# Moving one half tile's Relu and product into a later gate step of a fused state-space and ReGLU kernel

## The chip, the cores and the metric

The kernel runs on one core of a Trainium2 chip. The metric is the device time of one execution in microseconds. Three timed executions of the kernel before took 121.81, 121.49 and 121.47 us; their median is 121.49 us.

## The reference

Two stages follow each other. The first is a chunked state-space layer over `x` (4 batches, 8 heads, 768 positions, 32 channels) with a decay `a` and projections `B`, `C` of 16 states. For every chunk `c`:

```python
cum = np.cumsum(la, axis=-1)                       # la = log a of the chunk
M = (C_c @ B_c.T) * exp(cum_i - cum_j) * causal    # within the chunk
y = M @ x_c + (C_c @ state) * exp(cum)             # and from what came before
state = exp(sum la) * state + sum_j exp(cum_end - cum_j) * B_j x_j
```

The second stage takes the result as 3072 tokens of 256 channels through a gated feed-forward layer:

```python
gate = np.maximum(x @ w_gate, 0.0)     # 256 -> 1536
val = x @ w_val                        # 256 -> 1536
out = (gate * val) @ w_out             # 1536 -> 256
```

## The kernel before

The first stage works in pairs of 128-position chunks (256 tokens a pair, twelve pairs), the second in blocks of 512 tokens (two pairs a block, six blocks). A block has twelve gate steps `f`, one for each 128 columns of the 1536, and then output matmuls `o` (L810) that sum over the twelve. The work of both stages is woven together by hand: the order of the Python calls is the order on every engine's queue, and a last pass (`in_order`) pins each engine to it. There is no scheduler. What an instruction waits for follows from the tiles it reads and from the buffer it reuses.

A pair needs these steps. `transp` (L410) turns B and C, `bevac` and `cevac` (L415 to L436) copy them out of PSUM as `BT` and `CT`. `G` (L473) makes the products of C and B in four banks, and `gevac` copies them out with the causal mask: two of the copies by ScalarE (L486, L494), the rest by VectorE (L497). `back` (L454) turns `BT` back into a PSUM tile `bt`, in the bank that `transp` had used, so it waits until the last copy of `CT` has read that bank. `x_cast` makes `xb`, x in bf16. `astep` (L531) adds to the running state `A_ps`, `sevac` copies it out (`Sd`, L545, by ScalarE, or `carry` and `Sm`, L560 and L568, by VectorE). `Dm` (L652) multiplies the masked products with `xb`, `inter` (L632) adds the part of the state, and `yevac` writes the result `y` to `yT` in halves (ScalarE and VectorE).

A gate step of a whole block (`gv`, L765 to L769) is two matmuls into a bank `gate` and two into a bank `val`, a Relu by ScalarE (L768) that writes `r`, and a product by VectorE (L769) that writes a slice of `h`. Steps 0 to 3 of block 0 are done in halves of 256 tokens (`gvh_mm`, `gvh_relu`, `gvh_mul`, L780 to L792), with gate and val in one bank: the first halves (u = 0) while pair 1 is still in its first stage, the second halves (u = 1) as soon as pair 1 is in `yT`. Steps 4 to 11 follow as whole steps. Within step 5 comes `over_sum` (VectorE), after step 7 `sevac(1, 1)` (two VectorE instructions), after step 9 `turn` and `tevac` of pair 2 (PE transposes, one ScalarE copy, two VectorE scalings), after step 11 `back` of pair 2, and then the first output matmuls.

PSUM has eight banks. Five are shared by one pool tag and given to whatever asks next (`bank`); the tag "y" is a single bank, used by the warm-up matmuls, by the `y` of some pairs, and here by the half tile of step 0. The tile `r` has four buffers.

The lines that the change touches, in the order of the calls around them:

```python
gevac(1, early=True, between=lambda: backevac(1, nc.scalar))
gvh_relu(0, 0, 0)
for i in range(2):
    x_cast(1, i, nc.scalar)
```

Of the kernel before, what the change touches and what calls it, by code (L numbers as in the profile page):

```python
# [8 lines left out]
FP32 = mybir.dt.float32  # L9
# [20 lines left out]
def kernel(  # L30
# [31 lines left out]
    mm = ctx.enter_context(tc.tile_pool(name="mm", bufs=1, space=bass.MemoryType.PSUM))  # L62
# [3 lines left out]
    def bank(name="bank", shape=(128, 512), dtype=FP32):  # L66
        return mm.tile(list(shape), dtype, tag="shared", bufs=NSHARED, name=name)
# [89 lines left out]
    def w_tile(ws, f, k):  # L157
        return ws[f // 2][:, k, f % 2:256:2]
# [102 lines left out]
    def over_sum(de):  # L261
        own = smask.rearrange("p t (q d) -> p (t q) d", q=4)[:, :, 0]
        prod = const.tile([128, NB, 8], FP32)
        nc.vector.tensor_tensor(
            out=prod, in0=de.rearrange("p (b h) -> p b h", b=NB),
            in1=own.rearrange("p (o h) -> p o h", o=1).to_broadcast([128, NB, 8]),
            op=ALU.mult)
        nc.vector.tensor_reduce(out=over, in_=prod, op=ALU.add, axis=mybir.AxisListType.X)
# [187 lines left out]
    def backevac(p, eng):  # L456
        s = st[p]
        bx = att.tile([128, 2, 128], BF16, tag="bx", name="bx", bufs=4)
        copy(eng, bx, s.pop("bt"))
        s["B"] = [bx[:, i] for i in range(2)]  # L460
# [19 lines left out]
    def gevac(p, half=True, early=False, between=None, after={}):  # L480
        s = st[p]
        g = [t.rearrange("j i t m -> j (i t) m") for t in s["gp"]]
        d = s["gs"]
        wide = p < NWIDE
        m = masks[:, int(wide):int(wide) + 1].to_broadcast([128, 4, 128])
        nc.scalar.copy(out=d[:, 0], in_=g[0])  # L486
        causal(d[:, 0], 4, wide)
        if between:
            between()
        h = 2 if half else 0  # L490
        if early:
            nc.vector.tensor_tensor(out=d[:, 1, 0:2], in0=g[1][:, 0:2], in1=m[:, 0:2],
                                    op=ALU.mult)
        nc.scalar.copy(out=d[:, 1, h:4], in_=g[1][:, h:4])  # L494
        causal(d[:, 1, h:4], 4 - h, wide)
        for q in (2, 3):
            nc.vector.tensor_tensor(out=d[:, q], in0=g[q], in1=m, op=ALU.mult)  # L497
            if q in after:
                after[q]()
        if half and not early:  # L500
            nc.vector.tensor_tensor(out=d[:, 1, 0:2], in0=g[1][:, 0:2], in1=m[:, 0:2],
                                    op=ALU.mult)
# [19 lines left out]
    def astep(p, i):  # L522

        c = 2 * (p % PPB) + i
        if c == NC - 1:
            return
        if not A_ps:
            A_ps.append(mm.tile([128, 2, 128], FP32, tag="Aps", name="A_ps"))
        xi = st[p]["x"][i].rearrange("s (t q d) -> s q t d", t=2, q=4)
        for q in range(4):  # L530
            nc.tensor.matmul(  # L531
                out=A_ps[0][32 * q:32 * q + 32, 0, 0:64].rearrange("p (t d) -> p t d", t=2),
                lhsT=st[p]["B"][i][:, 32 * q:32 * q + 32], rhs=xi[:, q],
                start=(c == 0 or c == NC - 2), stop=True, tile_position=(0, 32 * q),
                skip_group_check=True)
# [3 lines left out]
    def sevac(p, i):  # L539
        c = 2 * p + i + 1  # L540
        if c == NC:
            return
        if c < 2 * NTILE:
            S[c] = n = att.tile([128, 64], BF16, tag="Sd", name="Sd")
            nc.scalar.copy(out=n, in_=A_ps[0][:, 0, 0:64])  # L545
        else:
            S[c] = spread_one(c, 0)
# [7 lines left out]
    def spread_one(c, k):  # L555

        b, a = c // NC, A_ps[0][:, 0, 64 * k:64 * k + 64]
        if c % NC == NC - 2:
            n = carried[b] = att.tile([128, 64], FP32, tag="carry", name="carry", bufs=2)
            nc.vector.tensor_scalar_mul(n, a, over[:, b:b + 1])  # L560
            a = n
        elif c % NC == NC - 1:
            n = att.tile([128, 64], FP32, tag="carry2", name="carry2", bufs=2)
            nc.vector.tensor_tensor(out=n, in0=a, in1=carried[b], op=ALU.add)
            a = n
        n = att.tile([128, 2, 128], BF16, tag="Sm", name="Sm", bufs=5)
        a = a.rearrange("p (t o d) -> p t o d", t=2, o=1)
        nc.vector.tensor_tensor(  # L568
            out=n.rearrange("p t (q d) -> p t q d", q=4),
            in0=a.to_broadcast([128, 2, 4, D]),  # L570
            in1=smask.rearrange("p t (q d) -> p t q d", q=4), op=ALU.mult)
        return n
# [91 lines left out]
    def yevac(p, *engs):  # L664
        s = st.pop(p)
        dst = yT[:, :, p * 256:(p + 1) * 256]
        if p >= NWIDE:
            copy(engs[0], dst.rearrange("q t (i m) -> q t i m", i=2), s["ya"])
            return
        for t in range(2):  # L670
            copy(engs[t % len(engs)],
                 dst[:, t].rearrange("q (i m r) -> q i r m", i=2, r=2),
                 s["y"][t].rearrange("q i (r m) -> q i r m", r=2))
# [84 lines left out]
    def gv(b, f, turns=False):  # L758
        if b not in fst:
            fst[b] = ffn.tile([128, NF, 512], BF16, tag="h", name="h")  # L760
        tk = slice(b * 512, (b + 1) * 512)
        g, v = bank("gate"), bank("val")
        order = [(g, wgs, 0), (g, wgs, 1), (v, wvs, 0), (v, wvs, 1)]
        for o, ws, k in sorted(order, key=lambda e: e[2]) if turns else order:
            nc.tensor.matmul(out=o, lhsT=w_tile(ws, f, k), rhs=yT[:, k, tk],  # L765
                             start=(k == 0), stop=(k == 1), skip_group_check=True)
        r = ffn.tile([128, 512], BF16, tag="r", name="r", bufs=4)
        nc.scalar.activation(r, g, AF.Relu)  # L768
        nc.vector.tensor_tensor(out=fst[b][:, f], in0=r, in1=v, op=ALU.mult)  # L769

    def gvh_mm(b, f, u):
        if f == 0 and u == 0:
            fst[b] = ffn.tile([128, NF, 512], BF16, tag="h", name="h")
        tk = slice(b * 512 + u * 256, b * 512 + (u + 1) * 256)
        gv_ = (mm.tile([128, 2, 256], FP32, tag="y", name="gv") if b + f == 0 else
               bank("gv", (128, 2, 256)))
        jk = [(j, k) for j in range(2) for k in range(2)]
        early = b + f + u == 0
        for j, k in sorted(jk, key=lambda v: v[1]) if early else jk:
            nc.tensor.matmul(out=gv_[:, j], lhsT=w_tile((wgs, wvs)[j], f, k), rhs=yT[:, k, tk],  # L780
                             start=(k == 0 and not (early and j)), stop=(k == 1),
                             skip_group_check=True)
        fst[b, f, u] = gv_

    def gvh_relu(b, f, u):
        fst[b, f, u, "r"] = r = ffn.tile([128, 512], BF16, tag="r", name="r", bufs=4)
        nc.scalar.activation(r[:, 0:256], fst[b, f, u][:, 0], AF.Relu)  # L787

    def gvh_mul(b, f, u):
        nc.vector.tensor_tensor(  # L790
            out=fst[b][:, f, u * 256:(u + 1) * 256], in0=fst.pop((b, f, u, "r"))[:, 0:256],
            in1=fst.pop((b, f, u))[:, 1], op=ALU.mult)  # L792
# [158 lines left out]
    G(1)  # L951
    back(1)
    gevac(1, early=True, between=lambda: backevac(1, nc.scalar))
    gvh_relu(0, 0, 0)
    for i in range(2):
        x_cast(1, i, nc.scalar)
    weights(3, (1,))
# [20 lines left out]
    inter(1, 0)  # L978
    inter(1, 1)
    astep(1, 1)  # L980
    gvh_mul(0, 0, 0)
    yevac(1, nc.scalar, nc.vector)
    gvh_relu(0, 2, 0)
    gvh_mm(0, 3, 0)
# [13 lines left out]
    for b in range(NBLK):  # L998
# [44 lines left out]
        for f in range(nh, NF):  # L1043
            gv(b, f, b > 2 and f == 0)
            if b == 0:
                if f == 5:
                    over_sum(de_ps)
                if f == 7:
                    sevac(1, 1)
                if f == 9:  # L1050
                    turn(P)
                    tevac(P, nc.scalar, nc.vector)
                if f == 10:
                    held(Q, bc=False)
                if f == 11:
                    back(P)
                    backevac(P, nc.scalar)
            elif b == 1:
                if f == 8:
                    scale_padded(Q + 1, nc.gpsimd)  # L1060
                    load(Q + 3, nc.sync)
            elif b == 2:
                if f == 9:
                    load(Q + 3, nc.sync)
            elif b == 3:
                if f in (2, 6):
                    scale(P + 2 + f // 4, nc.gpsimd)
# [142 lines left out]
```

## Time and profile before

| | |
|---|---|
| median of three runs | 121.49 us (121.47 to 121.81) |
| the profiled execution, its own time | 121.42 us |
| span from its first to its last instruction | 119.7 us |
| granted TensorE clock | 1.00 |
| busy: PE, VectorE, ScalarE, GpSimd | 96%, 73%, 64%, 43% of the span |

The time of an execution is 1.72 us above the span, which lies around the program's instructions. A row of the timeline has the start in us, the length in us, the engine, the line of the kernel, the operation, what is written from what is read, the shapes, and the number of instructions that the row merges; in brackets stands how long the engine was idle before and who released it. PEld is the loading of weights for PE. Instructions on one engine overlap: the next one starts before the one ahead has ended, so lengths do not add up and the distance between starts is what one costs.

### The profile page before, as it was taken

What the parts mean: (1) busy time and instruction counts of PE and PEld (TensorE: products, weight loads), DVE (VectorE), ACT (ScalarE), POOL (GpSimd) and SP (SyncE); (2) the same over time, 40 slices, a digit from 0 to 9 for tenths busy, and PEclk for the clock granted to TensorE, in tenths of its full rate; (3) what the DMA queues carried; (4) which work ended last, traced back from release to release, by engine and by line L of the source; (5) the groups of instructions that cost most, each with busy time, mean ns of one, the idle gap of its engine ahead of it and who ended that gap; (6) DMA issues with size and microseconds to landing.
All of it is one profiled execution on the core that took longest, in us unless ns stands there. A gap on an engine that the chain in (4) does not pass through costs nothing.

```text
span 119.7 us, 3291 instructions
## 1 busy us (share of the span) xinstructions
PE 115.0 (96%) x1222; PEld 74.6 (62%) x1229; DVE 87.1 (73%) x202; ACT 77.0 (64%) x168; POOL 51.2 (43%) x104
## 2 busy tenths in 40 slices
PE   7989999999999999999999999999999999999990
PEld 2446754677884577887578544578444677444790
DVE  6896779976898767899765778756787775678400
ACT  4288986777997635888627776535766445767240
POOL 7878999744413363957046635133400033000000
PEclk9999999999999999999999999999999999999999
DMA  3999999989999999999799999992200002200022
GB/s 67 212 176 182 203 198 205 202 121 129 93 117 132 144 127 135 101 104 177 72 175 118 97 128 218 267 312 93 88 0 5 0 0 93 88 0 0 0 88 88
DMA packets 82675, 14.22 MB, mean 119 GB/s; under 512 B 75500, under 2 KB 82660, under 8 KB 82660
## 3 DMA queue, kind: packets, MB, share of 16 engines
q1 hardware_dynamic: 75172, 11.07, 59.5%
q0 software_dynamic: 4080, 2.36, 14.0%
q10 hardware_dynamic: 3408, 0.59, 2.6%
q8 instruction: 9, 0.15, 0.5%
q14 instruction: 6, 0.05, 0.1%
HBM read 11.13 MB, written 3.15 MB: 119 GB/s over the span
## 4 chain that ended last, share of the span: by engine, by line
PE 95%; ACT 1%; issue 0%; DVE 0%
PE o L810 26%; PE gate L765 19%; PE val L765 19%; PE gv L780 14%; PE w L200 4%; PE g L513 2%; PE g L473 2%; PE y L705 1%; PE y L652 1%; PE o L822 1%; PE A_ps L237 1%; PE tp L410 1%; PE y L641 1%; ACT CT L434 1%; PE bt L454 1%; PE y L692 0%
## 5 line engine op out<-in xcount | busy, mean ns | idle before, releaser
L769 DVE TENSOR_TENSOR h<-r,val 128x512 bf16<-128x512 bf16 x54 | 36.9, 687 | 9.6 <-ACT r L768 7.5
L768 ACT ACTIVATE r<-gate 128x512 bf16<-128x512 f32 x54 | 32.3, 597 | 12.2 <-PE gate L765 11.7
L810 PE MATMUL o<-wo,h 128*128 128x256 bf16 x276 | 33.8, 273 | 0.0
L765 PE MATMUL gate<-yT,wg 128*128 128x512 bf16 x105 | 32.0, 379 | 0.2
L765 PE MATMUL val<-yT,wv 128*128 128x512 bf16 x105 | 31.5, 379 | 0.2
L810 PEld LDWEIGHTS <-h 128*128 128x128 bf16 x276 | 25.7, 98 | 5.4 <-issue 1.2
L171 POOL TENSOR_SCALAR_AFFINE_SELECT gs<-gs 128x512 bf16<-128x512 bf16 (+1 forms) x24 | 12.1, 527 | 28.4 <-ACT gs L486 28.4
L497 DVE TENSOR_TENSOR gs<-g,masks 128x512 bf16<-128x512 f32 x24 | 15.4, 685 | 5.9 <-PE g L513 2.8
L765 PEld LDWEIGHTS <-wv 128*128 128x128 bf16 x108 | 10.6, 98 | 12.4
L765 PEld LDWEIGHTS <-wg 128*128 128x128 bf16 x108 | 10.5, 98 | 11.5
L790 DVE TENSOR_TENSOR h<-r,gv 128x256 bf16<-128x256 bf16 x36 | 14.2, 417 | 1.3 <-ACT r L787 1.1
L787 ACT ACTIVATE r<-gv 128x256 bf16<-128x256 f32 x36 | 13.7, 390 | 1.2
L486 ACT CAST gs<-g 128x512 bf16<-128x512 f32 x12 | 7.0, 587 | 11.2 <-PE g L513 5.8
L780 PE MATMUL gv<-yT,wg 128*128 128x256 bf16 x72 | 13.9, 273 | 0.2 <-ACT yT L339 0.2
L780 PE MATMUL gv<-yT,wv 128*128 128x256 bf16 x72 | 13.8, 272 | 0.0
L842 ACT COPY ob<-o 128x512 f32<-128x512 f32 x11 | 6.5, 591 | 4.3 <-PE o L810 3.9
L299 POOL TENSOR_TENSOR bz<-bcr,fac 128x512 bf16<-128x512 f32 x6 | 6.4, 1060 | 5.6 <-PE gate L765 3.1
L339 ACT CAST yT<-y 128x256 bf16<-128x256 f32 (+1 forms) x11 | 5.4, 516 | 4.5 <-PE y L705 2.7
L780 PEld LDWEIGHTS <-wv 128*128 128x128 bf16 x72 | 7.0, 98 | 1.1 <-issue 0.3
L780 PEld LDWEIGHTS <-wg 128*128 128x128 bf16 x72 | 6.8, 98 | 1.0 <-issue 0.2
L339 POOL CAST xb<-xr 128x512 bf16<-128x512 f32 (+1 forms) x8 | 4.7, 591 | 4.2 <-DMA xr<-in_x_dram 4.0
L200 PE MATMUL w<-const-bfloat16-1.0 128*128 128x512 bf16 (+3 forms) x14 | 5.2, 498 | 0.8 <-PEq L1194 0.8
(120 smaller groups left out, 108.4 us busy)
## 6 DMA issues: line engine op xcount, KB each, us to landing
xr<-in_x_dram SPq DMA_DIRECT2D x24, 128.0 KB, 3.1
out_dram<-ob SPq DMA_DIRECT2D x11, 256.0 KB, 2.6
bcr<-in_B_dram SPq DMA_DIRECT2D x16, 64.0 KB, 2.9
bcr<-in_C_dram SPq DMA_DIRECT2D x16, 64.0 KB, 2.9
wg<-in_moe_w_gate_dram POOLq DMA_DIRECT2D x6, 128.0 KB, 4.5
wv<-in_moe_w_val_dram POOLq DMA_DIRECT2D x6, 128.0 KB, 4.7
wo<-in_moe_w_out_dram POOLq DMA_DIRECT2D x3, 256.0 KB, 6.8
bcr<-in_B_dram SPq DMA_DIRECT2D x3, 128.0 KB, 5.6
```

The lines of the kernel that those rows point to most:

```text
L171: nc.gpsimd.affine_select(out=dst, in_=dst, pattern=pattern, compare_op=ALU.is_ge, fill=0.0, base=0, channel_multiplier=-1)
L200: nc.tensor.matmul(out=w[:, 0:cols], lhsT=nc.const_aps.tensor(1.0, [128, 128], BF16), rhs=nc.const_aps.tensor(1.0, [128, cols], BF16), sta ...
L339: (eng.copy if eng is nc.scalar else eng.tensor_copy)(out=out, in_=in_)
L486: nc.scalar.copy(out=d[:, 0], in_=g[0])
L497: nc.vector.tensor_tensor(out=d[:, q], in0=g[q], in1=m, op=ALU.mult)
L765: nc.tensor.matmul(out=o, lhsT=w_tile(ws, f, k), rhs=yT[:, k, tk], start=(k == 0), stop=(k == 1), skip_group_check=True)
L768: nc.scalar.activation(r, g, AF.Relu)
L769: nc.vector.tensor_tensor(out=fst[b][:, f], in0=r, in1=v, op=ALU.mult)
L780: nc.tensor.matmul(out=gv_[:, j], lhsT=w_tile((wgs, wvs)[j], f, k), rhs=yT[:, k, tk], start=(k == 0 and not (early and j)), stop=(k == 1), ...
L787: nc.scalar.activation(r[:, 0:256], fst[b, f, u][:, 0], AF.Relu)
L790: nc.vector.tensor_tensor(out=fst[b][:, f, u * 256:(u + 1) * 256], in0=fst.pop((b, f, u, "r"))[:, 0:256], in1=fst.pop((b, f, u))[:, 1], op ...
L810: nc.tensor.matmul(out=o[:, ts % 2], lhsT=fst[b][:, f, ts * 128:(ts + 1) * 128], rhs=wo[:, f], start=(f == 0 and new), stop=(f == NF - 1), ...
```

## The change

Three things are edited. The Relu of the half tile (0, 0, 0) leaves its place ahead of the two casts of x of pair 1 and comes after step 7 of block 0; its product leaves its place ahead of the copy of `y` and comes after step 8. So that the half tile can keep the bank of the tag "y" until then, the second half of step 0 (u = 1) takes a shared bank instead of that one. No instruction is added or removed, and the order of PE's, GpSimd's and the DMA queues' instructions is the same.

```diff
-        gv_ = (mm.tile([128, 2, 256], FP32, tag="y", name="gv") if b + f == 0 else
+        gv_ = (mm.tile([128, 2, 256], FP32, tag="y", name="gv") if b + f + u == 0 else
                bank("gv", (128, 2, 256)))
...
     gevac(1, early=True, between=lambda: backevac(1, nc.scalar))
-    gvh_relu(0, 0, 0)
     for i in range(2):
         x_cast(1, i, nc.scalar)
...
     astep(1, 1)
-    gvh_mul(0, 0, 0)
     yevac(1, nc.scalar, nc.vector)
...
                 if f == 7:
                     sevac(1, 1)
+                    gvh_relu(0, 0, 0)
+                if f == 8:
+                    gvh_mul(0, 0, 0)
                 if f == 9:
                     turn(P)
                     tevac(P, nc.scalar, nc.vector)
```

## The prediction

> **What bounds the kernel now.** I read the page first, then the chain of waits, then the timeline around the two places that the edit touches, engine by engine.
>
> ```profile
> span 119.7 us, 3291 instructions
> PE 115.0 (96%) x1222; PEld 74.6 (62%) x1229; DVE 87.1 (73%) x202; ACT 77.0 (64%) x168; POOL 51.2 (43%) x104
> PE 95%; ACT 1%; issue 0%; DVE 0%
> 13.50:22.80 9.30, 9.25 (x59) 5.30 (x57) 8.43 (x21) 7.46 (x20) 9.30 (x14) 1.00 1.44 205
> ```
>
> TensorE is busy for 96% of the span and holds 95% of the chain that ended last. The last row is a stretch from the table by stages (length, then busy PE, PEld, DVE, ACT, POOL, the granted clock, DMA): through the gate steps of block 0 PE is busy 9.25 of 9.30 us at full clock. PE's order is not changed, so the question is only where PE would wait less and where it would wait more. What shifts PE here shifts the end, since I see nothing behind it that PE waits for long enough to absorb it. The first place is the end of pair 1's first stage:
>
> ```profile
> 11.44 0.39 ACT L494 CAST gs<-g 128x256 bf16<-128x256 f32 x1
> 11.70 0.41 ACT L787 ACTIVATE r<-gv 128x256 bf16<-128x256 f32 x1
> 11.98 0.73 ACT L339 CAST xb<-xr 128x256 bf16<-128x256 f32 x2
> 12.72 0.21 ACT L545 CAST Sd<-A_ps 128x64 bf16<-128x64 f32 x1
> 12.10 0.30 PEld L258 LDWEIGHTS dall<-pick,ends 96*128 96x128 f32 x2
> 12.44 0.11 PEld L531 LDWEIGHTS <-bx 128*32 128x32 bf16 x4
> 12.76 0.18 PEld L652 LDWEIGHTS <-xb 128*32 128x32 bf16 x12 [0.18 <-ACT xb L339]
> 12.46 0.21 PE L531 MATMUL A_ps<-xb,bx 128*32 128x64 bf16 x4
> 12.48 0.63 PE L652 MATMUL y<-gs,xb 128*32 128x128 bf16 x16
> 13.04 0.40 PE L632 MATMUL y<-CT,Sd 32*32 32x128 bf16 x16
> 13.50 0.45 DVE L339 CAST yT<-y 128x256 bf16<-128x256 f32 x1 [0.62 <-PE y L632]
> ```
>
> The Relu that moves is the second row. Behind it stand the two casts of x, which end at 11.98 + 0.73 = 12.71, and twelve of the sixteen weight loads of L652 wait for the second cast until 12.76. That is a real wait of PE on ScalarE. The second place is the end of the gate steps:
>
> ```profile
> 20.17 0.28 DVE L560 TENSOR_SCALAR carry<-A_ps,over 128x64 f32<-128x64 f32 x1
> 20.48 0.42 DVE L568 TENSOR_TENSOR Sm<-carry,smask 128x256 bf16<-128x256 f32 x1
> 20.83 1.28 DVE L769 TENSOR_TENSOR h<-r,val 128x512 bf16<-128x512 bf16 x2
> 22.02 0.60 DVE L436 TENSOR_SCALAR CT<-tp,tmask 128x256 bf16<-128x256 bf16 x2
> 22.54 0.68 DVE L769 TENSOR_TENSOR h<-r,val 128x512 bf16<-128x512 bf16 x1
> 22.41 0.10 PEld L765 LDWEIGHTS <-wv 128*128 128x128 bf16 x1
> 22.74 0.20 PEld L454 LDWEIGHTS <-BT 128*128 128x128 bf16 x2 [0.23 <-issue]
> 22.41 0.59 PE L765 MATMUL val<-yT,wv 128*128 128x512 bf16 x2
> 22.84 0.22 PE L454 MATMUL bt<-ident,BT 128*128 128x128 bf16 x1
> ```
>
> VectorE runs without an idle bracket from 20.17 on, and `bt` (L454) reuses the bank that the two scalings to `CT` read last; they end at 22.02 + 0.60 = 22.62. An undisturbed weight load starts together with the matmul ahead of it (22.41 and 22.41). The load for `bt` would by that start with the second val matmul, half of 22.84 - 22.41 after the first, at 22.63. It starts at 22.74, 0.12 after the scalings ended. It takes 0.10, and its matmul starts at 22.84, just when the pipe of matmuls is ready for it. So PE loses nothing there now, but has no margin left either.
>
> **The change part by part.**
>
> *The casts come earlier.* From the copy of G to the Relu ScalarE takes 11.70 - 11.44 = 0.26. The first cast takes the Relu's place at 11.70 and the pair ends at 11.70 + 0.73 = 12.43 instead of 12.71. The data must be there:
>
> ```profile
> 7.12 0.99 SPq L100 DMA_DIRECT2D xr<-in_x_dram  x2
> xr<-in_x_dram SPq DMA_DIRECT2D x2, 128.0 KB, 4.0
> ```
>
> The two loads are issued from 7.12 to 8.11 and take 4.0 to land, so the second is there at about 11.5, before the second cast would start near 12.0.
>
> *What PE makes of it.* L531 does not start earlier: its weights load at 12.44, right behind the loads of L258, which end at 12.10 + 0.30 = 12.40. The first four of L652 follow at 12.48, and the twelve others take to 12.48 + 0.63 = 13.11 from 12.76, 0.35 for twelve starts and one tail; four of them cost some 0.06. Without the wait the twelve would follow at 12.54 instead of 12.76: 0.22 gained. Not all is kept. The second half of L632 needs `Sd`, whose copy stands at 12.72 because L531 ends at 12.46 + 0.21 = 12.67, and that does not move; it ends at 12.93. With the 0.05 that the wait above shows between a ScalarE end (12.71) and the load it releases (12.76), the second half starts no earlier than 12.98. Now it starts about a third of the 0.40 behind 13.04, at 13.17. So the gain is 0.19; the ends are 0 (x lands late) and 0.22. `yevac` follows L632 (the DVE row at 13.50 waited for PE, not for its queue), and so do the next matmuls. I take 0.19, because each term has its own row.
>
> *The product leaves its old place.* It stood ahead of the copy at 13.50, before which VectorE was idle for 0.62. What goes from there was hidden and is worth nothing.
>
> *The bank of the second half tile.* With (0, 0, 0) holding the bank "y", the second half of step 0 takes the bank of `y0`, freed by the ScalarE copy whose result it needs anyway, and the later halves and step 4 each take a bank that comes free one product later than now. In the built program the tightest of these is the val bank of step 4, which now waits for the product of that second half, the first of four:
>
> ```profile
> 15.30 1.45 DVE L790 TENSOR_TENSOR h<-r,gv 128x256 bf16<-128x256 bf16 x4 [0.29 <-ACT r L787]
> L790 DVE TENSOR_TENSOR h<-r,gv x8: 361/417/422, 12.5 to 16.3; 128x256 bf16<-128x256 bf16 x8
> 16.15 0.59 PE L765 MATMUL val<-yT,wv 128*128 128x512 bf16 x2
> ```
>
> It ends near 15.30 + 0.42 = 15.72, and the val matmul starts at 16.15: 0.43 to spare, and both move with PE. Cost nothing; if that cover were gone, each 0.1 beyond it would be 0.1 on PE. From step 5 on the banks are waited for as now.
>
> *The Relu at its new place.*
>
> ```profile
> 18.94 0.60 ACT L768 ACTIVATE r<-gate 128x512 bf16<-128x512 f32 x1 [0.27 <-PE gate L765]
> 19.80 0.60 ACT L768 ACTIVATE r<-gate 128x512 bf16<-128x512 f32 x1 [0.27 <-PE gate L765]
> ```
>
> ScalarE is idle 0.27 ahead of each Relu. The moved one goes behind the Relu at 18.94 and ends at the latest at 18.94 + 0.60 + 0.41 = 19.95, so the Relu of step 8 slips by at most 0.15, from 19.80. It would end at 20.55, and its product starts only at 20.83, behind `carry` and `Sm`. Hidden by those two; nothing is charged.
>
> *The product at its new place.* This one is not hidden. It goes between the two products that the row at 20.83 merges, and pushes the second product, the scalings to `CT`, and what follows. Four such products took 1.45, so one costs (1.45 - 0.42) / 3 = 0.34 from start to start. The scalings end at 22.96 instead of 22.62 (before the shift of everything by the first gain), and `bt` starts at 23.18 instead of 22.84. PE stands still, for the wait is in its queue ahead of the output matmuls. If a little margin is left (at most the 0.12 between the scalings' end and the load, and I see 0.01 to 0.04 of it as free) the stall is smaller: I take 0.33, with ends 0.22 and 0.42. Next in line, nothing more is late: ScalarE's copy of `bt`, the transposes of pair 3 and the first output matmuls move with PE, the last two products by the same 0.34 as PE. The clear of `xr` behind them, which lets SP issue the loads of x of pair 3, moves too, by the net; SP's and POOL's orders are the same.
>
> The Trainium skill ("VectorE: DVE Perf Modes", section "The DRAIN you can't avoid") says that the next VectorE operation starts only when the pipe has emptied, unless it is one that is not held. By that the product would cost its full 0.42, the sum would be 0.09 higher, and the time 121.7; the rows disagree for this kind of instruction, as four took 1.45 and not 4 x 0.42 = 1.67.
>
> **The sum.** -0.19 + 0.33 = +0.14 us against the profiled execution's own 121.42, whose span is 119.7: 121.56. That execution lies 0.07 under the median of the runs, so against 121.49 it is 121.63; I say 121.6. A measurement of this kernel can tell about 0.3% (0.36 us) from no change, so this counts as no change.
>
> **The rivals.**
>
> *The wait at `bt` finds cover (121.3).* If the load at 22.74 was late for another reason than the scalings (the profile puts its idle 0.23 down to "issue", not to VectorE, which speaks for it), the 0.34 is partly hidden, and the gain in front stays: -0.19 at best, 121.3. Against it: the load for `bt` is the one in that stretch that starts late, and it does so 0.12 behind the scalings. This ends within 0.3% too.
>
> *Slower (121.8 to 121.9).* The gain in front does not come, because x of pair 1 is not there when ScalarE is ready. The place is the first cast; the point from which it decides is a landing after 11.98, half a microsecond later than here. Then only the stall remains: +0.33, up to +0.42 with the product at full length, 121.82 to 121.91. For it: the DMA engines are fully busy in these microseconds (the share in the stage's row, 1.44, counts overlapping packets), and 4.0 us to land is a single execution's value. Against it: here the landing leaves 0.2 to 0.5. The same time would come from any second wait of 0.2 or more on PE behind the late products.
>
> *Faster by more than 0.3% (121.0 to 121.1).* The moved Relu's whole 0.41 was on the path, and the stall is covered: -0.41, 121.08. It takes L531 to move with the casts, against the loads of L258 that hold it at 12.40, and `Sd` with it.
>
> **How the numbers follow.** I give the forecast 0.50, the covered wait 0.12, slower 0.26, faster 0.12. The forecast and the covered wait are both within 0.3% of 121.49 (121.13 to 121.85): 0.62. The range of eight in ten cuts the far end of the fast rival and leaves 0.1 above the slow one: 121.1 to 122.0. The likeliest case alone, with the stall's ends 0.22 and 0.42 and the gain's 0.19 to 0.22, spans 121.5 to 121.7.
>
> **What would show it.** Right: the casts of x start at 11.7, the wait of L652 for ScalarE is gone, and gate step 4 starts some 0.19 earlier; the scalings to `CT` end about 0.34 later against the gate matmuls, and PE has a gap of about 0.33 ahead of `bt`, after which all of PE runs 0.14 later than before. Wrong: L652 still waits for the casts; or no gap ahead of `bt`; or a second gap, at the first transposes of pair 3, at G of pair 2, or where a bank is not free between 14 and 17 us.

## The result, and the profile after

The changed kernel took 122.01 us (median of 13 runs, 121.60 to 122.33); the kernel before took 121.50 us in the 13 runs beside them (121.08 to 121.81). The ratio is 1.0038, with a 95% interval of 1.0023 to 1.0054. It is slower, by about 0.46 us where I had worked out 0.14. On the median of 121.49 the ratio gives 121.95, inside the range of 121.1 to 122.0, near its upper end; the outcome that I held likeliest, no change within 0.3%, was not quite met. The same kernel measured a second time, below, came out at 1.0013 (0.9988 to 1.0038). All ratios and intervals are of executions in the fast state; in the series below a few executions were in a slower one, by up to 4%, and are left out.

The profiled execution of the changed kernel took 121.97 us. First its page: the span, and the chain that ended last by engine.

```profile
span 120.3 us, 3289 instructions
PE 93%; ACT 2%; DVE 1%; issue 1%
```

The span is 0.6 longer, and ScalarE and VectorE hold a little more of the chain: 2% and 1%, where they had 1% and 0%. (The two records fewer are not among the instructions that the pages count as busy; these are the same in number on every engine.) Now the timeline of the first place, ScalarE's rows and then PE's:

```profile
11.43 0.39 ACT L494 CAST gs<-g 128x256 bf16<-128x256 f32 x1
11.69 0.73 ACT L339 CAST xb<-xr 128x256 bf16<-128x256 f32 x2
12.70 0.21 ACT L545 CAST Sd<-A_ps 128x64 bf16<-128x64 f32 x1 [0.28 <-PE A_ps L531]
12.44 0.21 PE L531 MATMUL A_ps<-xb,bx 128*32 128x64 bf16 x4
12.48 0.40 PE L652 MATMUL y<-gs,xb 128*32 128x128 bf16 x16
12.80 0.45 PE L632 MATMUL y<-CT,Sd 32*32 32x128 bf16 x16
13.19 0.21 PE L531 MATMUL A_ps<-xb,bx 128*32 128x64 bf16 x4
```

The casts start at 11.69, the sixteen matmuls of L652 take 0.40 instead of 0.63, `Sd` stays where it was (12.70 against 12.72) and holds L632, and the next L531 starts at 13.19 instead of 13.38. That is the 0.19 of the prediction, of which 0.02 stood already at the L531 ahead (12.44 against 12.46). The second place, VectorE's rows and then those of PE and its weight load:

```profile
18.26 0.20 DVE L264 TENSOR_TENSOR prod<-dall,smask 128x32 f32<-128x32 f32 x1
18.49 0.19 DVE L268 TENSOR_REDUCE over<-prod 128x4 f32<-128x32 f32 x1
18.98 1.28 DVE L769 TENSOR_TENSOR h<-r,val 128x512 bf16<-128x512 bf16 x2 [0.31 <-PE gate L765]
20.18 0.28 DVE L560 TENSOR_SCALAR carry<-A_ps,over 128x64 f32<-128x64 f32 x1
20.50 0.42 DVE L568 TENSOR_TENSOR Sm<-carry,smask 128x256 bf16<-128x256 f32 x1
21.44 0.41 DVE L790 TENSOR_TENSOR h<-r,gv 128x256 bf16<-128x256 bf16 x1
22.36 0.60 DVE L436 TENSOR_SCALAR CT<-tp,tmask 128x256 bf16<-128x256 bf16 x2
22.23 0.59 PE L765 MATMUL val<-yT,wv 128*128 128x512 bf16 x2
23.08 0.13 PEld L454 LDWEIGHTS <-BT 128*128 128x128 bf16 x2 [0.76 <-ACT r L768]
23.11 0.27 PE L454 MATMUL bt<-ident,BT 128*128 128x128 bf16 x2 [0.29 <-ACT r L768]
24.10 0.39 PE L410 MATMUL tp<-ident,bs 128*128 128x128 bf16 x4
24.47 0.38 PE L810 MATMUL o<-wo,h 128*128 128x256 bf16 x2
```

The moved product stands at 21.44, the scalings to `CT` start at 22.36 instead of 22.02, and PE waits ahead of `bt`. From the start of the last val pair to `bt` PE's pace needs 22.84 - 22.41 = 0.43, as before; now it is 23.11 - 22.23 = 0.88. So PE loses 0.45 there, not 0.33. (Name and length in the bracket are the profile's guess; I go by the starts.) The main reason is in the third row: VectorE is idle for 0.31 ahead of the product of step 6. Up to there it was 0.19 ahead of the kernel before, like PE (18.49 against 18.68 at L268); behind it `carry` starts at 20.18, and before it stood at 20.17. So VectorE lost there what it had gained, and PE had not.

A part of what VectorE loses does not reach PE. In nine of the thirteen traces of this case PE waits ahead of `bt`, and in each of them the load of its weights starts 0.12 after the scalings' end and the matmul 0.03 after that load, 0.15 in all; here at 22.97, 23.08 and 23.11. In the kernel before, the load also started 0.12 after the scalings, but the matmul 0.10 after the load, at PE's own pace. The scalings could have ended 0.07 later without delaying it: there was a margin of 0.07.

Two smaller losses come later. In the kernel before, the transposes at L410 and the ninth output matmul, and L652 and L591, followed each other like this:

```profile
23.83 0.39 PE L410 MATMUL tp<-ident,bs 128*128 128x128 bf16 x4
24.05 0.38 PE L810 MATMUL o<-wo,h 128*128 128x256 bf16 x2
28.12 0.40 PE L652 MATMUL y<-gs,xb 128*32 128x128 bf16 x16
28.34 0.26 PE L591 MATMUL A_ps<-xb,bx 128*32 128x64 bf16 x12
```

0.22 lies between the starts of each pair. In the changed kernel the first pair is 24.47 - 24.10 = 0.37 apart; the second is

```profile
28.53 0.40 PE L652 MATMUL y<-gs,xb 128*32 128x128 bf16 x16
28.94 0.27 PE L591 MATMUL A_ps<-xb,bx 128*32 128x64 bf16 x12
28.27 0.62 ACT L339 CAST xb<-xr 128x512 bf16<-128x512 f32 x1 [0.45 <-DMA xr<-in_x_dram]
L161 POOL DMA_DIRECT2D wo<-in_moe_w_out_dram x3: 756/761/768, 15.9 to 17.3; - x3
DMA to landing us min/median/max: 6.4/7.8/8.3
```

0.41 apart, since L591 waited for the cast of x of pair 3, and that for its loads. The second of these was issued at 24.0 instead of 23.7, since the clear of `xr` that releases it moved from 23.16 to 23.50, and it took 4.1 to land instead of 3.3. By my estimate the 0.19 needed both, the later release (0.35) and the longer landing (0.8): had either been as before, the cast, for which ScalarE stood ready 0.45 earlier, would have ended before L591 could start. The ninth output matmul needs the second of the three loads of `wo`: issued near 16.6, and landed 7.8 later by the median, at 24.4; in the kernel before the median was 6.8, at 23.4. So this execution's account is -0.19 + 0.45 + 0.15 + 0.19 = +0.60, which is what the spans differ by.

### The profile page after: what moved, and what is told of

It reads as the page before. It is cut to its first block, busy times and chain, and to the rows that moved or that the text cites. A ratio compares the mean times of both kernels' runs of the same rounds, so it can differ in the third digit from the quotient of the medians.

```text
span 120.3 us, 3289 instructions
## 1 busy us (share of the span) xinstructions
PE 114.8 (95%) x1222; PEld 74.4 (62%) x1229; DVE 87.2 (72%) x202; ACT 76.9 (64%) x168; POOL 50.6 (42%) x104
## 4 chain that ended last, share of the span: by engine, by line
PE 93%; ACT 2%; DVE 1%; issue 1%
PE o L810 26%; PE gate L765 19%; PE val L765 19%; PE gv L780 14%; PE w L200 3%; PE g L513 2%; PE g L473 2%; PE y L705 1%; PE y L652 1%; PE o L822 1%; PE A_ps L237 1%; DVE bs L365 1%; PE bt L454 1%; PE y L641 1%; ACT CT L434 1%
## 5 line engine op out<-in xcount | busy, mean ns | idle before, releaser
L339 DVE CAST yT<-y 128x512 bf16<-128x512 f32 (+1 forms) x5 | 3.0, 595 | 3.8 <-PE y L705 1.9
```

The costliest lines, as they stand in the source:

```text
L339: (eng.copy if eng is nc.scalar else eng.tensor_copy)(out=out, in_=in_)
```

## The experiments

My theory was the prediction's: the gain in front is real, and the late product makes PE wait at `bt`. Its rivals were that the late Relu or the late loads make the loss, and that the loss is not made by the edit's order at all. Each kernel was timed beside runs of the kernel before on the same chip; there were three chips. In these series the times of one kernel lie up to 1.8 us apart, so that a ratio can hardly tell less than 0.3% from nothing; where a gap on PE is the question, I go by the trace. In six of the executions PE also waited once near 51 us for a late load, a place that no edit touches:

```profile
51.52 0.23 PE L720 MATMUL A_ps<-xb,bz 128*32 128x64 bf16 x8
52.90 0.24 PE L720 MATMUL A_ps<-xb,bz 128*32 128x64 bf16 x8 [1.15 <-POOL xb L339]
```

These two rows are from the next kernel; they make up most of the 1.8 us by which its span is longer than that of the kernel before.

**The front alone.** The kernel before, with the Relu behind the casts and the product where it was.

```diff
-    gvh_relu(0, 0, 0)
     for i in range(2):
         x_cast(1, i, nc.scalar)
+    gvh_relu(0, 0, 0)
```

> The kernel before with one edit: the half tile's Relu goes behind the two casts of x of pair 1, and its product stays at its old place. If the gain in front is what the trace of the changed kernel shows (PE 0.195 us earlier from the second half of L632 on), and nothing at bt takes it back, PE is 0.19 earlier up to the end: 121.3 us, ratio 0.9984. If PE's earlier start is taken back by something that does not move with it (weights landing, VectorE), the ratio is 1.000 and the shift of PE is gone by 23 us.

Ratio 0.9989 (0.9960 to 1.0018). In its trace PE starts the whole stretch 0.12 later than in the trace of before (the first G of pair 1), yet reaches `bt` at 22.78 instead of 22.84, without a wait: 0.18 gained. It then loses 0.47 at the transposes of pair 3 (24.24 - 22.78 = 1.46 behind `bt` instead of 0.99), where PE waits for GpSimd's scaling, which a late load of B held until 22.99. It was run twice more:

> The kernel before with the Relu behind the two casts of x and the product at its old place, once more. If the gain in front stays where no late product takes it back: PE 0.19 earlier at bt, and a ratio of 0.998 to 0.999 where the transposes of pair 3 do not wait for a late load; 1.000 where they do.

> The casts first and the product at its old place, nothing else, a third time and beside the run above: ratio 0.998 to 1.000. Where GpSimd's scaling of pair 3 falls on the copy Sm of VectorE, that copy takes longer than 0.42 and bt is late by as much less what margin is left; where it does not, bt is 0.19 earlier or at its pace.

Ratios 0.9987 (0.9963 to 1.0012) and 1.0027 (0.9996 to 1.0059). The gain at L632 is there each time; but `bt` was late by 0.17 and 0.19 in these two traces, although no product had been moved. Here are VectorE and GpSimd in the first of the two:

```profile
20.41 0.67 DVE L568 TENSOR_TENSOR Sm<-carry,smask 128x256 bf16<-128x256 f32 x1
22.20 0.60 DVE L436 TENSOR_SCALAR CT<-tp,tmask 128x256 bf16<-128x256 bf16 x2
19.60 1.19 POOL L365 TENSOR_TENSOR bs<-bcr,wfac 128x256 bf16<-128x256 f32 x2 [0.20 <-DMA bcr<-in_B_dram]
```

`Sm` took 0.67 instead of 0.42 while GpSimd scaled pair 3 beside it. Of these 0.25 all but the margin of 0.07 arrived at PE. So the front gains 0.17 to 0.19 in these traces, but what becomes of it by the end was not measured clear of zero.

**The late product alone.** The changed kernel with the Relu back in front, in a buffer `r` of its own.

```diff
     def gvh_relu(b, f, u):
-        fst[b, f, u, "r"] = r = ffn.tile([128, 512], BF16, tag="r", name="r", bufs=4)
+        fst[b, f, u, "r"] = r = (
+            ffn.tile([128, 512], BF16, tag="r0", name="r0", bufs=1) if b + f + u == 0 else
+            ffn.tile([128, 512], BF16, tag="r", name="r", bufs=4))
...
+    gvh_relu(0, 0, 0)
     for i in range(2):
         x_cast(1, i, nc.scalar)
...
                     sevac(1, 1)
-                    gvh_relu(0, 0, 0)
                 if f == 8:
                     gvh_mul(0, 0, 0)
```

> The changed kernel with the Relu back at its early place (in a buffer r of its own), so that only the product is late. If the product alone delays the scalings to CT by 0.34, PE stalls ahead of bt by 0.30 to 0.35 against the kernel before, without a gain in front, and the two later shifts that the changed kernel showed (0.15 at the second third of the output matmuls, 0.18 at the states of pair 3) come on top if they follow from it: 121.8 to 122.2, ratio 1.003 to 1.006. If the late Relu on ScalarE was what hurt, the ratio is 1.000.

Ratio 1.0024 (0.9993 to 1.0055), just under the expected 1.003 to 1.006 and not clear of 1. From the val pair to `bt` it takes 22.96 - 22.08 = 0.88: the same stall of 0.45 as in the changed kernel, more than the expected 0.30 to 0.35. So the late Relu on ScalarE does not make the stall; the product does. Neither of the two later losses is in this trace.

**Another bank for `bt`.** The changed kernel, with `bt` of pair 2 in a shared bank.

```diff
-        s["bt"] = (mm.tile([128, 2, 128], BF16, tag="tp", name="bt") if p else
+        s["bt"] = (mm.tile([128, 2, 128], BF16, tag="tp", name="bt") if p not in (0, 2) else
                    bank("bt", (128, 2, 128), BF16))
```

> The changed kernel with bt of pair 2 in a shared bank instead of the bank that the scalings to CT read, so that its wait for them is gone. If that wait is where the changed kernel loses, the gap of PE ahead of bt closes and 0.46 of shift is gone at 23 us; the output matmuls start 0.19 earlier than in the kernel before. The time is 121.3 to 121.6 (ratio 0.998 to 1.001), the upper end if the later shifts of 0.15 and 0.18 stay. If the loss is made by the loads of x of pair 3 and the landing of the third weights alone, the ratio stays at 1.003 to 1.004.

PE's rows, and GpSimd's:

```profile
22.26 0.59 PE L765 MATMUL val<-yT,wv 128*128 128x512 bf16 x2
22.69 0.28 PE L454 MATMUL bt<-ident,BT 128*128 128x128 bf16 x2
22.80 1.04 PE L810 MATMUL o<-wo,h 128*128 128x256 bf16 x8
24.45 0.34 PE L410 MATMUL tp<-ident,bs 128*128 128x128 bf16 x3 [0.62 <-POOL bs L365]
23.20 1.19 POOL L365 TENSOR_TENSOR bs<-bcr,wfac 128x256 bf16<-128x256 f32 x2 [3.87 <-DMA bcr<-in_B_dram]
```

The gap ahead of `bt` is gone (0.43 from val to `bt`), and the output matmuls start at 22.80, 0.16 earlier than in the kernel before. So the wait for the scalings is what stops PE. But the ratio is 1.0034 (1.0002 to 1.0066): in this execution a load of B of pair 3 landed late, GpSimd scaled it only at 23.20, and PE waited 0.62 at the next transposes. The expectation for the gap was met, that for the time was not.

**The product behind the scalings.** The changed kernel, with the product two instructions later on VectorE.

```diff
-                if f == 8:
-                    gvh_mul(0, 0, 0)
...
                     tevac(P, nc.scalar, nc.vector)
+                    gvh_mul(0, 0, 0)
```

> The changed kernel with the product behind the two scalings to CT instead of ahead of them. The scalings are then not delayed, but the clear of xr behind the product, which releases the loads of x of pair 3, still is, by 0.34. If the wait at bt is what costs, PE has no gap ahead of bt and the time falls to 121.3 to 121.5 (ratio 0.998 to 1.000). If the late clear and the loads behind it cost the 0.18 seen at the states of pair 3, that shift stays in the trace, and the ratio is 1.000 to 1.001.

Ratio 0.9994 (0.9961 to 1.0026). From val to `bt` it takes 22.54 - 22.01 = 0.53, so 0.10 is left of the 0.45. The first output matmul starts at 22.78 instead of 22.65, since the product that it reads ended only at 22.31 + 0.41 = 22.72. Moving the product by two instructions takes most of the stall away, as the theory says. What is left goes with the idle time ahead of the product of step 6, which stands in this trace too (0.28). PE waited 0.43 more at the transposes of pair 3, as in the experiment above. And the front gained only 0.05 here (0.87 from the first L531 to the next; 0.92 in the kernel before, 0.75 in the changed one): the load of x of pair 1 took 4.9 to land, and the second cast started 0.55 behind the first instead of 0.31.

**The changed kernel again.**

> The changed kernel once more, unedited. The steps that follow from the order of its instructions must come again in another trace: the casts 0.28 earlier, a gap of about 0.29 on PE ahead of bt, and the idle 0.31 on VectorE ahead of the product of step 6, which no wait in the trace explains. The later shifts, at the ninth output matmul (0.15) and at the states of pair 3 (0.18), and the one at 24.2 us that other kernels showed at the transposes of pair 3, depend on when loads land and may differ. Ratio 1.001 to 1.005.

Ratio 1.0013 (0.9988 to 1.0038). The idle time ahead of the product of step 6 is there again, and PE waits even longer:

```profile
18.96 1.29 DVE L769 TENSOR_TENSOR h<-r,val 128x512 bf16<-128x512 bf16 x2 [0.30 <-PE gate L765]
20.48 0.90 DVE L568 TENSOR_TENSOR Sm<-carry,smask 128x256 bf16<-128x256 f32 x1
19.90 1.20 POOL L365 TENSOR_TENSOR bs<-bcr,wfac 128x256 bf16<-128x256 f32 x2 [0.61 <-DMA bcr<-in_B_dram]
22.22 0.59 PE L765 MATMUL val<-yT,wv 128*128 128x512 bf16 x2
23.57 0.27 PE L454 MATMUL bt<-ident,BT 128*128 128x128 bf16 x2 [0.76 <-DVE CT L436]
```

`Sm` took 0.90 beside GpSimd's scaling, and the stall is 23.57 - 22.22 - 0.43 = 0.92. The two later losses, at the ninth output matmul and at L591, are absent, in part because PE comes to both places later here. They are not fixed consequences of the change.

**One more instruction on VectorE.** The unexplained idle time of about 0.3 stood in every kernel with the late product. In the trace of the changed kernel the last wait of that instruction had ended by 18.52, and it started at 18.98. It differs from the kernel before in the bank that it reads and in its number: one VectorE instruction fewer stands ahead of it. This kernel restores the number alone:

```diff
     astep(1, 1)
+    nc.vector.memset(first[:, 0:1], 0.0)
     yevac(1, nc.scalar, nc.vector)
```

> The changed kernel with a clear of one word on VectorE at the place where the moved product stood, so that the number of VectorE instructions ahead of step 6 is that of the kernel before, while the banks are those of the changed kernel. If the idle 0.31 ahead of the product of step 6 comes from how many instructions stand before it, it is gone, the scalings to CT end 0.2 earlier, and the gap of PE ahead of bt falls from 0.46 (against PE's pace) to about 0.27. If it comes from the bank that this product reads, or from anything else of the changed order, it stays at 0.3. Ratio 0.999 to 1.003 in the first case, that of the changed kernel in the second.

```profile
18.48 0.19 DVE L268 TENSOR_REDUCE over<-prod 128x4 f32<-128x32 f32 x1
18.59 1.48 DVE L769 TENSOR_TENSOR h<-r,val 128x512 bf16<-128x512 bf16 x2
22.23 0.60 DVE L436 TENSOR_SCALAR CT<-tp,tmask 128x256 bf16<-128x256 bf16 x2
22.22 0.59 PE L765 MATMUL val<-yT,wv 128*128 128x512 bf16 x2
22.98 0.27 PE L454 MATMUL bt<-ident,BT 128*128 128x128 bf16 x2 [0.16 <-DVE CT L436]
```

The idle time is gone: the product starts at 18.59, 0.39 earlier, and `carry` at 19.98 instead of 20.18. (Only 0.20 is left there, since the product of step 7 now waits for its Relu: 1.48 for the two products instead of 1.28.) From val to `bt` it takes 0.76, a stall of 0.33, and `bt` stands at 22.98 against 22.84: +0.14. Both are the prediction's figures, but by luck: `Sm` took 0.49 here, 0.07 longer than in the kernel before, which makes up for the margin of 0.07 that the prediction did not count. With `Sm` at 0.42 the stall would be 0.26, by my estimate. The ratio is 1.0004 (0.9979 to 1.0030). The number of instructions, not the bank, made the idle time.

**One fewer in the kernel before.** The converse: one clear of a constant at the very start goes from VectorE to GpSimd.

```diff
-    nc.vector.memset(zero1, 0.0)
+    nc.gpsimd.memset(zero1, 0.0)
```

> The kernel before with one clear of a constant (zero1, at the very start) given to GpSimd, so that one VectorE instruction fewer stands ahead of step 6, as in the changed kernel, and nothing else differs. If the idle 0.3 ahead of the product of step 6 comes from that number, it now stands in the kernel before too; the scalings to CT end some 0.2 later and PE starts bt 0.15 to 0.2 later than its pace: ratio 1.001 to 1.002. If the number has nothing to do with it, there is no such idle time and the ratio is 1.000.

```profile
18.52 0.19 DVE L268 TENSOR_REDUCE over<-prod 128x4 f32<-128x32 f32 x1
19.00 1.28 DVE L769 TENSOR_TENSOR h<-r,val 128x512 bf16<-128x512 bf16 x2 [0.30 <-PE gate L765]
22.26 0.59 PE L765 MATMUL val<-yT,wv 128*128 128x512 bf16 x2
22.81 0.27 PE L454 MATMUL bt<-ident,BT 128*128 128x128 bf16 x2
```

The idle 0.30 now stands in the kernel before, and `bt` is 0.55 - 0.43 = 0.12 late, a little less than the expected 0.15 to 0.20: against the last val pair the scalings start 0.19 later (22.06 against 22.26; in the kernel before 22.02 against 22.41), and 0.07 of that is covered by the margin. The ratio, 1.0006 (0.9972 to 1.0040), can't tell 0.12 us from nothing.

**The loads of x of pair 3 earlier.** The changed kernel, with the clear that releases them ahead of the product.

```diff
                 if f == 8:
+                    held(Q, bc=False)
                     gvh_mul(0, 0, 0)
...
-                if f == 10:
-                    held(Q, bc=False)
```

> The changed kernel with the clear that releases the loads of x of pair 3 ahead of the late product instead of two VectorE instructions behind the scalings to CT, so that these loads are issued 1.5 to 2 us earlier. If their late landing made the last 0.18 of the changed kernel's loss, PE does not wait at the states of pair 3 and the ratio against the changed kernel is 0.998 to 0.999. If that wait is not there on this chip anyway, or the earlier loads only crowd out others, the ratio is that of the changed kernel. The gap ahead of bt stays in both cases.

Ratio 1.0007 (0.9984 to 1.0031) against the kernel before; against the repeat of the changed kernel, which ran beside it, that is 0.9994, within the noise. L591 does not wait, but it did not in that repeat either, so this does not settle what the late clear costs. The second load was issued at 22.2 instead of 24.5, but took 5.8 to land instead of 3.3, and so came no earlier. The stall at `bt` is 23.30 - 22.33 - 0.43 = 0.54.

**Casts first and another bank for `bt`.** Both single edits shown above, together.

> The casts first, the product at its old place, and bt of pair 2 in a shared bank, which frees it from the scalings to CT (it then waits for the product of step 9, two instructions earlier on VectorE). If PE has no margin against VectorE at bt, this keeps the gain in front whatever VectorE does there: bt 0.19 earlier and a ratio of 0.998 to 0.999. If the next wait, at the transposes of pair 3 for GpSimd's late scaling, comes right behind, that gain is lost there and the ratio is 0.999 to 1.000.

PE is at its pace at `bt` (0.43), which stands 0.03 earlier than in the kernel before although this execution entered the stretch 0.15 later; so the gain in front is kept there, as expected. The profiled execution then waits 0.38 at L720 for a late load. The ratio is 1.0010 (0.9979 to 1.0042), above the 0.998 to 0.999 that I expected, with both inside the interval. No version measured clearly faster than the kernel before.

## Why the prediction was right or wrong

*The casts and what PE makes of them.* Right, in place and nearly in size: the casts start at 11.69 against the 11.70 of the prediction, the next L531 comes 0.19 earlier, held there by `Sd`, and gate step 4 too (15.53 against 15.71). Of the 0.19 the edit's own part is 0.17, since 0.02 stood there before the casts.

*Old place of the product, the bank of the second half tile, the Relu at its new place.* Nothing was charged, and no wait appears at any of the three. The bank is cleared by the kernel with one more instruction, which has the changed banks and no new stall but the one at `bt`. But the old place was not quite worth nothing: with the product one instruction goes from VectorE's queue, and that is what the idle time ahead of step 6 hangs on.

*The product at its new place.* The mechanism was right: the scalings to `CT` come later, and PE waits for them ahead of `bt`. Another bank took the gap away, and moving the product behind the scalings took 0.35 of its 0.45. The size was off, 0.45 instead of 0.33 and beyond the upper end of 0.42, and two terms of the sum were wrong in opposite directions. The first is the shift of VectorE ("before the shift of everything by the first gain"): the idle time put it back by 0.20 against PE, and the prediction had no such term. The second is the margin ("has no margin left either"): the prediction took it that the matmul needs the whole 0.10 of the load, but it started 0.03 after the load wherever PE waited, so that 0.07 was free. The product's own 0.33 was right (21.77 - 21.44). Together these give 0.33 + 0.20 - 0.07 = 0.46, the measured 0.45 but for rounding. Without the idle time the two places would have come to -0.19 + 0.26 = +0.07, by my estimate, and not to the +0.14 of the sum.

*"Next in line, nothing more is late."* Not so in the first trace: 0.15 and 0.19 were lost to loads of `wo` and x that landed late. The loads of `wo` were issued when they were before, so nothing ties their landing to the edit; the loads of x were released 0.35 later by it, but cost 0.19 only together with their longer landing. Since the repeat did not show either loss, they are not settled as part of the change. With 0.26 from the two places that the edit touches (-0.19 + 0.45), and an interval for the whole of 0.28 to 0.66 us in the first series and of -0.15 to +0.46 in the second, some of the first series' loss stays open. That `Sm` lengthens to 0.90 beside GpSimd in the repeat shows one way in which the late product can cost more in one execution than in another; how often it does was not measured.

*The rivals.* The covered wait at `bt` did not come: the load does wait for the scalings, and the cover is the 0.07. The slow rival gave the right neighbourhood of times for a wrong reason: in the changed kernel's trace x of pair 1 was there. (In one experiment it was late, and most of the gain went.) Its last sentence, any second wait on PE, came nearer. The fast rival is out: L531 did not move with the casts (12.44 against 12.46). That the time fell inside the range was luck in part: the range reached that far up for the slow rival, and the time got there by the idle time on VectorE, which the prediction did not have, and by loads that landed late.

## What to carry to other kernels

Before moving work to an engine that looks idle on average, look for a consumer with no margin at the end of that engine's dense stretch: one small operation of 0.33 us on VectorE went through to TensorE but for a margin of 0.07, and so did every other disturbance of VectorE ahead of it. Measure such a margin where the consumer does wait, in another trace if need be, before taking it for nothing. A saving in one place need not reach every engine, so write down each engine's own shift up to the place in question. And when a gap of a few tenths of a microsecond has no wait behind it, restore the instruction count with a tiny dummy before blaming banks or data.

## What the runs showed of the hardware

VectorE stood idle for 0.28 to 0.31 us, with all its waits over, ahead of one instruction, the product of step 6. It did so in all seven traces in which one instruction fewer stood ahead of it, across two programs that were otherwise the changed and the unchanged kernel, and in none of the six with the original number. In the seven the product is the 64th record of VectorE in the trace, counting the waits that the trace records; in the six it is the 65th, and the 64th, one of these waits, shows no such delay. So the runs tie the idle time to the count, but the count alone is not the rule; what in the engine makes it, and whether it comes back at later counts under other work, was not tried.

The VectorE operation `Sm`, which reads and writes SBUF alone, and GpSimd's scaling of pair 3, which does so too, held each other up. Where no operation of the scaling was running when `Sm` began, `Sm` took 0.42 or 0.43. In six traces one was running. In one of these it ended 0.11 later, and `Sm` took its 0.42; in the other five `Sm` ended 0.27 or 0.28 after that operation, and took 0.49, 0.52, 0.67, 0.69 and 0.90. In the trace of the late product alone `Sm` began first, at 20.34, and took its 0.42, and the GpSimd operation that began at 20.45 took 0.79 instead of 0.68. So it looks as if the later of the two waits for the earlier one to end; no experiment was made for it.
